# Linear attention into an ELU feed-forward, one core: first products of four chunks, two more pairs transposed by DMA, one set of PSUM banks, and a new order of work

## The chip, the cores and the metric

The kernel runs on one core of one Trainium2 chip. The metric is the device time of one execution in microseconds (us), the median of several runs. TensorE (PE) multiplies matrices from SBUF into PSUM, which has eight banks; VectorE (DVE) and ScalarE (ACT) read PSUM and write SBUF; GpSimd (POOL) computes in SBUF and issues the loads that change the type; SyncE (SP) issues the other transfers, the stores and the transposes by DMA.

## The reference

Four sequences of 768 tokens with eight heads of 64 go through a linear attention with decay, in blocks; its output, 3072 rows of 512, goes through two dense layers with an ELU between them. Cut to what matters:

```python
intra = einsum('bhic,bhjc->bhij', qb, kb) * Dmask          # scores within a block, masked by decay
intra = einsum('bhij,bhjd->bhid', intra, vb)
inter = einsum('bhid,bhde->bhie', qb * lam_pow, kv_state)   # what earlier blocks left
out   = intra + inter
kv_state = lam_block * kv_state + einsum('bhsd,bhse->bhde', kb * rev_pow, vb)
...
x = out.transpose(0, 2, 1, 3).reshape(B * S, H * D)         # 3072 x 512
h = x @ w_in                                                # 512 x 2048
g = where(h > 0, h, exp(min(h, 0)) - 1)
return g @ w_out                                            # 2048 x 512
```

## The kernel before

**The pieces.** The work is cut into 24 chunks of 128 tokens. Chunk g is block g // 4 of sequence g % 4, so chunk g needs the state that chunk g - 4 left. Everything is multiplied in float16 and summed in PSUM in float32.

**The order.** A long string, PROGRAM, holds one word for each step, and the loop at line 453 carries the words out one after another. Since each engine works through its own instructions in order, the words of one engine make that engine's queue. The text behind an @ names the PSUM bank or banks that the word takes. The words, with the chunk numbers behind the letters:

- Lq, Lk, Lv (load, line 238): POOL issues the load of one chunk, or from chunk 4 on of a pair, from float32 in memory to float16 in SBUF. wi and wo (lines 244, 250) load a block of 256 columns of the first weight, or 256 rows of the second, eight of each. Hq and Hk (line 225) load a chunk as float32 over SP's queue, and Cq or Ck (line 231) casts it.
- T, Tq, Tk (transpose, line 259): TensorE transposes q and k of a chunk, four matmuls for each against the identity; tq (DVE, which also multiplies by the decay qs) and tk (ACT, unless named in ON) copy the result to qT and kT. Dq and Dk (transpose_dma, line 278): SP issues a DMA that does the same without TensorE, DVE or ACT; the decay qs then comes in later, in p.
- S (scores, line 282): the scores of a chunk, 16 small matmuls in two banks; s (masked, line 292): DVE multiplies one half by the mask.
- P (products, line 298): masked scores times values plus q times state, in one bank; p (evacuate_p, line 315) copies it to xt, the input of the dense layers: on ACT if q came by tq, on DVE with the factor qs if it came by Dq.
- kd (POOL) and U (TensorE) make what a chunk adds to the state, M (POOL) decays the old state, u (DVE) adds the two.
- A (first_product, line 385): 128 x 512 of the first dense layer's output, in a bank. x (ACT) takes the exponential of it, r (ACT) the maximum with 0 in place, m (DVE) puts the two together as g. A chunk has 2048 columns of hidden layer. A group of n chunks shares its A words: four words for each chunk alone (16 matmuls of 128 columns each), eight words for a pair (eight matmuls of 256 columns each). GROUPS names the groups.
- B (second_product, line 416): a quarter of the second dense layer of one chunk, four matmuls of 512 columns; o copies the sum to osb, st (SP) stores it. Of the last chunk, 384 columns go this way and the last 128 in R, oR and stR.

**The banks.** Before, A takes the two buffers of bank H in turn; scores, products, updates and transposes share A, B, C, D; the second products take M0 and M1, and now and then another word takes one of these.

**The order around the change.** Chunks 0 to 3 go alone. T4 to T7 stand on TensorE, with their copies on DVE and ACT. Words A and B alternate from the start: the first A is A0:0, the first B is B0:0, two A later. Around the first product of chunk 4 the order reads:

```
B2:3 A3:1 S4@M0,B M4 Lk10 S5@A,M1 Lq10 M5 s4.0 s5.1 s4.1 x3:1 A3:3 o2 x3:3 s5.0 kd7 r3:3
T6@D B3:0@M0 P4@C P5@B p4 p5 m3:3 B3:3 A4:0 r3:1 Lv6 tk6 m3:1 tq6 Dq8 Dq9 Dk9 x4:0 r4:0
```

POOL's loads stand in this order: wi1, then q, k, v of the first chunks with wi0, wo0, wo1, wi2, wi3 among them, then the other weights, then Lq4 Lk4 Lk6 Lq6 Lv4 Lq8 and so on. A tile's buffers (BUFS) bound how far a load can run ahead: four for each of q, k, v in pairs, five for qT and for kT, 40 for g.

Of the kernel before, what the change touches and what calls it, by code (L numbers as in the profile page):

```python
# [11 lines left out]
ALU = mybir.AluOpType  # L12


GROUPS = [(0, 1), (1, 1), (2, 1), (3, 1), (4, 2), (6, 2), (8, 2), (10, 2), (12, 2), (14, 2), (16, 2), (18, 2), (20, 2), (22, 2)]

LOADS = [(0, 1), (1, 1), (2, 1), (3, 1), (4, 2), (6, 2), (8, 2), (10, 2), (12, 2), (14, 2), (16, 2), (18, 2), (20, 2), (22, 2)]

BUFS = {'qn1': 4, 'kn1': 4, 'vn1': 4, 'qn2': 4, 'kn2': 4, 'vn2': 4, 'qT': 5, 'kT': 5, 'pp': 6, 'kd': 8, 'stt': 8, 'xt1': 4, 'xt2': 2, 'xt4': 2, 'e': 3, 'g': 40, 'osb512': 4}

ON = {'z0.0', 'z2.0', 'z1.0', 'o23', 'z3.0'}

# [4 lines left out]


PROGRAM = (
# [53 lines left out]
)  # L85


# [1 line left out]
def kernel(  # L89
# [11 lines left out]
    nc = tc.nc  # L101
# [57 lines left out]
        return sb.tile(shape, dtype, tag=tag, name=name, bufs=BUFS.get(tag, 1))  # L159

    def bank(tag, shape, dtype, name):
        return ps.tile(shape, dtype, tag=f"ps{tag}", name=name, bufs=2 if tag == "H" else 1)

    def ln(_):
        nc.scalar.activation(loglam[:], lam_b[:], AF.Ln)
# [216 lines left out]
                out=new, in0=stt.pop((g, hh))[r], in1=psU.pop((g, hh)), op=ALU.add  # L382
            )

    def first_product(g0, j):
        n = size_of[g0]
        assert {f"p{g0 + i}" for i in range(n)} <= done
        pH = psH[g0, j] = bank("H", [128, FB * 128], FP32, f"psH{g0}_{j}")
        for f in range(FB // n):
            i, w = divmod(j * (FB // n) + f, 2)  # L390
            for kk in range(NHP):
                nc.tensor.matmul(  # L392
                    pH[:, f * n * 128 : (f + 1) * n * 128],
                    lhsT=wi16[i][:, kk, w * 128 : (w + 1) * 128],
                    rhs=xg[g0][:, kk, :], start=(kk == 0), stop=(kk == NHP - 1),
                )
# [38 lines left out]
        t0 = b * S + c * L  # L435
        nc.sync.dma_start(out=out[t0 : t0 + 128, cols], in_=osb.pop((g, cols.start))[:])

    rest = []

    def last_columns(banks):  # L440
        cols = slice(CUT, DM)
# [11 lines left out]
    for word in words:  # L453
# [17 lines left out]
        elif kind in ("Dq", "Dk"):  # L471
            transpose_dma(kind[1], *a)
        elif kind == "S":
            scores(*a, banks)
        elif kind == "P":
            products(*a, banks)
        elif kind == "U":
            update_products(a, banks)
        elif kind == "B":
            second_product(*a, banks)  # L480
        elif kind == "o":
            evacuate_o(*a, psM.pop(*a)[:, cols_of(*a)], cols_of(*a), name in ON)
        elif kind == "st":
            store(*a, cols_of(*a))
        elif kind == "R":
            last_columns(banks)
        elif kind == "oR":
            evacuate_o(LAST, rest[0][:], slice(CUT, DM), False)
        elif kind == "stR":
            store(LAST, slice(CUT, DM))  # L490
        else:
            {
                "wi": load_wi, "wo": load_wo, "z": zero_state, "s": masked, "p": evacuate_p,
                "kd": decay_k, "M": decay_state, "u": update, "A": first_product, "x": exp,
                "r": relu, "m": elu,
            }[kind](*a)

# [29 lines left out]
```

## Time and profile before

| what | value |
|---|---|
| median of 3 runs (lowest to highest) | 215.63 us (215.39 to 217.02) |
| the profiled execution | 215.01 us |
| its span, first to last instruction | 213.2 us |
| granted clock of TensorE, mean | 1.000 |
| first matmul, first A | 6.13 us, 14.39 us |
| x, mean of 96, ACT (line 400) | 596 ns |
| r, mean of 96, ACT (line 403) | 594 ns |
| m, mean of 96, DVE (line 408) | 685 ns |
| s, mean of 48, DVE (line 294) | 682 ns |
| transposes by DMA, issue to landing, median | 5.1 us for qT, 4.1 us for kT |
| loads of a pair, POOL's issue, mean | 1.1 us |

The span is what the trace covers; the device time is some 1.8 us longer. Busy times of TensorE are modelled ends of matmuls that overlap, so the cost of a matmul is read from the distance between starts: a chain entry such as "16 matmuls in 1.75 us" gives it, the mean duration does not. A DMA share over 1 means that more than one packet was under way on each engine.

### The profile page before, as it was taken

The numbers are of one execution on the slowest core, as the hardware profiler recorded it, in microseconds if no ns is written. First come the engines' busy times: TensorE is split into PE (matmuls) and PEld (weight loads), VectorE is DVE, ScalarE is ACT, GpSimd is POOL, SyncE is SP. The second block draws the span as 40 slices with busy tenths as digits, with TensorE's granted clock in tenths as the row PEclk, the third lists the DMA queues.
The fourth block names the chain that finished last, engine by engine and source line by source line (L and its number), as shares of the span: only waits on it lengthen the run. The fifth ranks groups of instructions, "written<-read, shape, count | busy, mean of one in ns | idle before, by whom it ended". The sixth has DMA issues, their size and how long they took to land.

```text
span 213.2 us, 5052 instructions
## 1 busy us (share of the span) xinstructions
PE 199.2 (93%) x2048; PEld 138.5 (65%) x2048; DVE 129.6 (61%) x223; ACT 127.9 (60%) x245; POOL 96.6 (45%) x115
## 2 busy tenths in 40 slices
PE   0599989999999999999989999999999999999994
PEld 0378767677677766767657677667666776666662
DVE  3877764385877866788538676366558665353321
ACT  4436766568776765585554865665674565556731
POOL 7999965599994995376902691000000000000000
PEclk9999999999999999999999999999999999999999
DMA  5999999999999999969997999146110000021042
GB/s 95 152 181 184 197 194 182 158 145 151 161 120 166 127 169 150 148 101 113 187 148 80 158 187 127 25 130 145 25 52 0 0 16 36 3 103 46 0 152 98
DMA packets 101976, 24.59 MB, mean 115 GB/s; under 512 B 92608, under 2 KB 99008, under 8 KB 101952
## 3 DMA queue, kind: packets, MB, share of 16 engines
q0 software_dynamic: 79760, 13.50, 83.5%
q1 hardware_dynamic: 22192, 10.76, 23.9%
q8 instruction: 16, 0.26, 0.5%
q14 instruction: 8, 0.07, 0.1%
HBM read 27.27 MB, written 6.29 MB: 157 GB/s over the span
## 4 chain that ended last, share of the span: by engine, by line
PE 64%; POOL 17%; DMA 15%; issue 1%; ACT 0%; SPq 0%; POOLq 0%
PE psM L422 29%; PE psH L392 28%; DMA kn<-in_k_dram 5%; DMA vn<-in_v_dram 4%; DMA qT<-qn 4%; POOL wi L245 3%; POOL kn L240 3%; POOL wo L251 3%; POOL kd L332 3%; DMA out_dram<-osb 3%; POOL qn L240 3%; PE psO L304 2%; POOL vn L240 2%; PE psO L310 2%; PE psS L287 2%
## 5 line engine op out<-in xcount | busy, mean ns | idle before, releaser
L408 DVE SCALAR_TENSOR_TENSOR g<-e,psH 128x512 f16<-128x512 f32 x96 | 65.6, 685 | 61.3 <-ACT psH L403 61.0
L392 PE MATMUL psH<-xt,wi 128*128 128x256 f16 (+1 forms) x896 | 97.6, 259 | 0.9 <-DMA wi<-in_moe_w_in_dram 0.8
L400 ACT ACTIVATE e<-psH 128x512 f32<-128x512 f32 x96 | 57.2, 596 | 67.4 <-PE psH L392 67.0
L422 PE MATMUL psM<-wo,g 128*128 128x512 f16 (+1 forms) x384 | 92.7, 377 | 0.2 <-ACT osb L431 0.2
L392 PEld LDWEIGHTS <-wi 128*128 128x128 f16 x896 | 77.5, 99 | 22.8 <-DMA wi<-in_moe_w_in_dram 1.3
L403 ACT ACTIVATE psH<-psH 128x512 f32<-128x512 f32 x96 | 56.9, 594 | 0.0
L422 PEld LDWEIGHTS <-g 128*128 128x128 f16 x384 | 36.4, 98 | 31.4 <-issue 0.4
L294 DVE TENSOR_TENSOR pp<-psS,mask 128x512 f16<-128x512 f32 x48 | 31.4, 682 | 7.6 <-PE psS L287 7.5
L332 POOL TENSOR_TENSOR kd<-kn,ks 128x512 f16<-128x512 f16 x20 | 20.8, 1049 | 13.0 <-DMA kn<-in_k_dram 12.5
L342 POOL TENSOR_TENSOR stt<-st,upp 64x256 f32<-64x256 f16 x32 | 19.6, 612 | 7.4 <-DVE st L381 5.9
L240 POOL DMA_DIRECT2D vn<-in_v_dram x14 | 15.7, 1121 | 9.0 <-PE psO L310 9.0
L431 ACT COPY osb<-psM 128x512 f32<-128x512 f32 x23 | 13.4, 588 | 5.7 <-PE psM L422 4.8
L240 POOL DMA_DIRECT2D kn<-in_k_dram x14 | 15.5, 1107 | 1.6 <-DMA wi<-in_moe_w_in_dram 1.4
L240 POOL DMA_DIRECT2D qn<-in_q_dram x13 | 14.4, 1110 | 0.1
L381 DVE TENSOR_TENSOR st<-stt,psU 64x256 f16<-64x256 f32 x32 | 13.0, 415 | 0.8 <-PE psU L366 0.3
L304 PE MATMUL psO<-pp,vn 128*64 128x128 f16 x192 | 12.5, 229 | 0.3 <-DMA vn<-in_v_dram 0.3
L304 PEld LDWEIGHTS <-vn 128*64 128x64 f16 x192 | 10.0, 114 | 2.6 <-issue 1.6
L328 DVE TENSOR_TENSOR xt<-psO,qs 128x512 f16<-128x512 f32 x16 | 10.7, 683 | 1.1 <-PE psH L392 0.6
L287 PE MATMUL psS<-qT,kT 64*128 64x128 f16 x192 | 8.4, 228 | 2.8 <-DMA qT<-qn 1.1
L310 PE MATMUL psO<-qT,st 128*64 128x128 f16 x160 | 10.3, 219 | 0.0
L287 PEld LDWEIGHTS <-kT 64*128 64x128 f16 x192 | 5.9, 98 | 5.8 <-issue 3.6
L310 PEld LDWEIGHTS <-st 128*64 128x64 f16 x160 | 9.0, 110 | 0.0
(45 smaller groups left out, 65.1 us busy)
## 6 DMA issues: line engine op xcount, KB each, us to landing
out_dram<-osb SPq DMA_DIRECT2D x23, 256.0 KB, 2.9
qn<-in_q_dram POOLq DMA_DIRECT2D x10, 256.0 KB, 8.0
kn<-in_k_dram POOLq DMA_DIRECT2D x10, 256.0 KB, 6.5
vn<-in_v_dram POOLq DMA_DIRECT2D x10, 256.0 KB, 7.0
wi<-in_moe_w_in_dram POOLq DMA_DIRECT2D x8, 256.0 KB, 6.4
wo<-in_moe_w_out_dram POOLq DMA_DIRECT2D x8, 256.0 KB, 7.4
kn<-in_k_dram POOLq DMA_DIRECT2D x4, 128.0 KB, 4.7
vn<-in_v_dram POOLq DMA_DIRECT2D x4, 128.0 KB, 5.5
```

The lines of the kernel that those rows point to most:

```text
L240: nc.gpsimd.dma_start(out=t[:].rearrange("p b h d -> p (b h) d"), in_=source(w, g0, load_n[g0]))
L287: nc.tensor.matmul(psS[g, hh][:, hp, :], lhsT=tr["k", g][r, hp, :], rhs=tr["q", g][r, hp, :], start=True, stop=True,)
L294: nc.vector.tensor_tensor(out=p[:], in0=psS.pop((g, hh))[:], in1=mask[:, hh::2, :], op=ALU.mult)
L304: nc.tensor.matmul(po[r, hp, :], lhsT=of("v", g)[:, 2 * hp + hh, :], rhs=pp[g, hh][:, hp, :], start=True, stop=(cb == 0), skip_group_check ...
L310: nc.tensor.matmul(po[r, hp, :], lhsT=st[b][cb % 2][:, hp, r], rhs=tr["q", g][:, hp, :], start=False, stop=True, skip_group_check=True,)
L332: nc.gpsimd.tensor_tensor(out=kds[g][:], in0=of("k", g), in1=ks[:].unsqueeze(2).broadcast_to([128, H, 64]), op=ALU.mult,)
L342: nc.gpsimd.tensor_tensor(out=t[r], in0=st[b][cb % 2][r, :, r], in1=upp[r].unsqueeze(2).broadcast_to([64, NHP, 64]), op=ALU.mult,)
L392: nc.tensor.matmul(pH[:, f * n * 128 : (f + 1) * n * 128], lhsT=wi16[i][:, kk, w * 128 : (w + 1) * 128], rhs=xg[g0][:, kk, :], start=(kk = ...
L400: nc.scalar.activation(es[g0, j][:], psH[g0, j][:], AF.Exp)
L403: nc.scalar.activation(psH[g0, j][:], psH[g0, j][:], AF.Relu)
L408: nc.vector.scalar_tensor_tensor(out=g[:].rearrange("p f c t -> p (f c t)"), in0=es.pop((g0, j))[:], scalar=-1.0, in1=psH.pop((g0, j))[:], ...
L422: nc.tensor.matmul(psM[g][:, cols], lhsT=gts[g, f], rhs=wo16[i][:, w, cols], start=f == 0, stop=f == NFT - 1, skip_group_check=True,)
```

## The change

- GROUPS: from chunk 8 on, four chunks share their first product (16 words A for a group, four matmuls of 512 columns each) instead of two. Chunks 0 to 3 stay alone, 4 to 7 stay pairs.
- Chunks 4 to 7: the words T, tq and tk are replaced by Dq and Dk. Their p goes from ACT to DVE, since the factor qs now comes in there.
- Banks: every bank is a single buffer, named 0 to 7, and every A names its bank.
- Head: a word wz sets a tile of zeros, and 14 words W multiply zeros, 13 ahead of the first transposes and one behind Tq1. Chunk 0's k comes over SP as float32 (Hk0, Ck0).
- The order of all words is new.

```diff
-GROUPS = [(0, 1), (1, 1), (2, 1), (3, 1), (4, 2), (6, 2), (8, 2), (10, 2), (12, 2), (14, 2), (16, 2), (18, 2), (20, 2), (22, 2)]
+GROUPS = [(0, 1), (1, 1), (2, 1), (3, 1), (4, 2), (6, 2), (8, 4), (12, 4), (16, 4), (20, 4)]
...
-ON = {'z0.0', 'z2.0', 'z1.0', 'o23', 'z3.0'}
+WARM = [512, 512, 512, 512, 512, 512, 512, 512, 512, 512, 512, 512, 512, 512]
+
+ON = {'z3.0', 'z0.0', 'z2.0', 'o23', 'Ck0', 'z1.0'}
...
-        return ps.tile(shape, dtype, tag=f"ps{tag}", name=name, bufs=2 if tag == "H" else 1)
+        return ps.tile(shape, dtype, tag=f"ps{tag}", name=name, bufs=1)
...
-    def first_product(g0, j):
+    def first_product(g0, j, banks):
...
-        pH = psH[g0, j] = bank("H", [128, FB * 128], FP32, f"psH{g0}_{j}")
+        pH = psH[g0, j] = bank(banks[0], [128, FB * 128], FP32, f"psH{g0}_{j}")
...
+    def make_zeros(_):
+        idle.append(const("zeros", [128, 512], FP16))
+        nc.vector.memset(idle[0][:], 0.0)
+
+    def zeros_product(k, banks):
+        if k == 0:
+            idle.append(bank(banks[0], [128, 512], FP32, "psW"))
+        nc.tensor.matmul(
+            idle[1][:, : WARM[k]], lhsT=idle[0][:, :128], rhs=idle[0][:, : WARM[k]],
+            start=True, stop=True,
+        )
```

The new order from the head to the first products of chunk 4, and its end; the middle is left out:

```
Hq0 wz W0@0 W1 W2 W3 W4 W5 wi3 W6 W7 W8 W9 W10 Lq1 iota row z3.1 pos0 idn Lk2 Lk1 Lq2 tab
lam ln Cq0 Hk0 W11 W12 pos1 dn Ck0 Tk0@1 Lk3 Lv1 Lq3 Lv2 Lv0 wi2 wi0 wi1 llp qs up pos2
Tq0@2 ks z0.0 tk0 kd1 kd0 Lv3 wi4 wi5 wi6 wo1 kd3 wi7 cau wo0 Lq4 Lk4 wo4 wo5 Lk6 wo3 wo2
Dq5 Dq4 Lq6 Tq1@3 W13 tq0 tq1 wo6 z2.1 Tk2@4 tk2 msk S0@5,6 s0.1 Tk1@7 tk1 S1@0,2 Tq2@1 tq2
S2@3,4 T3@7 U1@6 s0.0 s1.1 tk3 s2.0 s2.1 P2@1 P0@5 s1.0 z1.1 tq3 kd2 U0@2 wo7 p2 p0 P1@3 p1
z3.0 S3@4,0 Dk5 A2:1@1 x2:1 r2:1 A0:1@7 A1:1@5 x1:1 s3.0 m2:1 A1:0@3 s3.1 x1:0 r1:0 Dk4 P3@4
u1.0 A2:0@1 m1:0 u1.1 A0:0@0 Dk6 Dk7 p3 Dq6 A3:1@4 x0:1 r0:1 m0:1 r1:1 x0:0 m1:1 r0:0 x2:0
Dq7 A0:2@3 z0.1 u0.1 A1:2@6 Lv4 A3:0@7 U3@5 r2:0 m2:0 u0.0 x1:2 r1:2 m1:2 A2:2@1 x0:2 r0:2
x3:0 m0:2 r3:0 A3:2@2 m3:0 m0:0 x2:2 kd7 r2:2 m2:2 A0:3@6 x0:3 r0:3 m0:3 u3.1 A1:3@3 A3:3@7
x3:3 z1.0 A2:3@0 r3:3 m3:3 u3.0 Lk8 kd5 M5 x2:3 B1:0@1 B0:0@6 B2:0@7 B2:2 r2:3 m2:3 B1:2
x1:3 r1:3 x3:2 r3:2 m3:2 Lv6 kd6 M4 B3:0@5 B3:2 B0:2 m1:3 B1:1 x3:1 r3:1 m3:1 U2@0 u2.1 B3:1
u2.0 B2:1 B0:1 S5@2,3 S4@4,0 B1:3 B0:3 s5.0 s4.1 s4.0 s5.1 B3:3 Lq8 Lq10 kd4 P4@2 p4 P5@0 p5
U4_5@4 B2:3 M6 A4:4@3 u5.1 u5.0 u4.1 Lk10 o0 o2 M7 Lv8 u4.0 x4:4 o3 A4:1@6 x4:1 r4:1 o1 r4:4
...
A20:8@2 B20:1 B20:3 B23:3 x20:8 r20:8 m20:8 B21:2 o21 B22:2 o22 st22 B20:2 o20 st21 B23:2 st20 o23
st23 R@0 oR stR
```

In the middle, the scores of chunks 8 to 11 stand between B of chunks 4 to 7, those of 12 to 15 among the A of the group at 8, and those of 16 to 23 among the A of the group at 12 and the B of chunks 8 to 11. The 16 A of the groups at 16 and 20 come last, mixed with each other and with B of chunks 12 to 19. TensorE's queue has 32 transposing matmuls fewer, SP's has eight transposes more (40 instead of 32).

More of the change, by code (lines that the diff above doesn't have):

```diff
@@ L436, in store @@
         nc.sync.dma_start(out=out[t0 : t0 + 128, cols], in_=osb.pop((g, cols.start))[:])
-    rest = []
+    rest, idle = [], []
+    def make_zeros(_):
+        idle.append(const("zeros", [128, 512], FP16))
+        nc.vector.memset(idle[0][:], 0.0)
+    simple["wz"] = make_zeros
+    def zeros_product(k, banks):
[5 more added lines that the diff above has]
+        )
     def last_columns(banks):
@@ L478 @@
             update_products(a, banks)
+        elif kind == "A":
+            first_product(*a, banks)
+        elif kind == "W":
+            zeros_product(*a, banks)
         elif kind == "B":
@@ L493 @@
                 "wi": load_wi, "wo": load_wo, "z": zero_state, "s": masked, "p": evacuate_p,
-                "kd": decay_k, "M": decay_state, "u": update, "A": first_product, "x": exp,
+                "kd": decay_k, "M": decay_state, "u": update, "x": exp,
                 "r": relu, "m": elu,
```

109 rows, old and new, of the table PROGRAM are left out of this document.

## The prediction

> **What bounds the kernel now.** I read five views: the busy table, the chain of waits, the timeline of TensorE, the windows of the DMA-heavy stretch, and the timeline of SP's queue. The busy table first.
>
> ```profile
> PE 199.2 (93%) x2048; PEld 138.5 (65%) x2048; DVE 129.6 (61%) x223; ACT 127.9 (60%) x245; POOL 96.6 (45%) x115
> ```
>
> TensorE is the bound on average, so the question is what one of its words costs and where it stands still. The chain of waits gives the prices (start, length, what), and two landings.
>
> ```profile
> 28.72 11.07 DMA kn<-in_k_dram
> ...
> 50.37 7.86 DMA vn<-in_v_dram
> ...
> 83.00 1.73 PE psM L422 x8
> 84.73 1.75 PE psH L392 x16
> ...
> 209.22 0.91 PE psMrest L445 x16
> ```
>
> 16 matmuls of 256 columns take 1.75 us (109 ns each), 8 of 512 columns 1.73 us (216 ns each), 16 of 128 columns 0.91 us (57 ns each). So a word B costs 0.863, a two-chunk A (eight matmuls) 0.872, a one-chunk A (sixteen of 128 columns) 0.90. The keys of chunks 4 and 5 (Lk4) landed at 39.8, the values of 6 and 7 (Lv6) at 58.2. The timeline shows where TensorE starts, where chunk 4's output product P4 begins, and its named stops behind that.
>
> ```profile
> 14.39 2.80 PE L392 MATMUL psH<-xt,wi 128*128 128x128 f16 x31
> ...
> 46.96 0.25 PE L304 MATMUL psO<-pp,vn 128*64 128x128 f16 x2
> ...
> 58.28 0.25 PE L304 MATMUL psO<-pp,vn 128*64 128x128 f16 x2 [0.33 <-DMA vn<-in_v_dram]
> ...
> 107.48 0.62 PE L287 MATMUL psS<-qT,kT 64*128 64x128 f16 x16 [1.09 <-DMA qT<-qn]
> ```
>
> Behind 14 us TensorE hardly rests, and what stops it is DMA. The windows (last three columns: clock, DMA share, GB/s) and SP's queue show the DMA side.
>
> ```profile
> 30.00:36.00 6.00, 5.22 (x70) 3.95 (x69) 1.77 (x4) 3.85 (x9) 3.42 (x3) 1.00 1.48 194
> 36.00:42.00 6.00, 6.00 (x62) 4.00 (x60) 2.55 (x6) 3.04 (x7) 2.14 (x2) 1.00 2.45 158
> ...
> 46.59 3.09 SPq L280 DMA_TRANSPOSE qT<-qn  x2
> 49.77 2.60 SPq L280 DMA_TRANSPOSE kT<-kn  x2
> 55.33 6.61 SPq L280 DMA_TRANSPOSE qT<-qn  x3
> ```
>
> From 36 to 42 us only loads of pairs of chunks run: 262 KB at 158 GB/s is 1.66 us each. Weights go at 194 GB/s, 1.35 us each. The share is over 1, so the DMA engines are full: there is a second bound, as high as TensorE, to some 60 us.
>
> **The change part by part.**
>
> *Four chunks at a time.* From chunk 8 on, 64 two-chunk A words (0.872) become 64 four-chunk words of four 512-column matmuls (0.864): 0.5 us less. The number of x, r and m is the same (96 each, by 128x512 rows), so ACT and DVE gain nothing.
>
> *Chunks 4 to 7 by DMA.* TensorE loses 32 transposes of 57 ns, 1.8 us. ACT loses four tk and four p, 8 x 0.59; DVE swaps four tq for four p. SP gains eight transposes, which it issues at about 1.3 us each, and the DMA engines move them while full. Their price: from Lk4 (39.8) to Lv6 (58.2) nine pair loads landed. At 1.66 us they need 14.9 of the 18.4; 3.5 us went to the four or five transposes that ran in that time, 0.7 to 0.9 each. I take 0.8. From below the bound is 0 (they hide); from above 1.3, SP's issue time, if loads stop whenever SP transposes.
>
> *Head.* The key of chunk 0 goes over SP as float32 (256 KB, 1.35 us at the weights' rate) instead of over POOL (128 KB, 0.83): 0.5 more of DMA. POOL issues two loads before the iota where it was one, so row, identity and qs come about 0.9 later (mean of such an issue 1.1, the first ones 0.9). All four chunks' scores come before the first A: DVE has 7.9 us of work from the first tq to the first A, before 6.7. Together 0.9 + 1.2 + 0.7 for the two casts and later qs on ACT: the first A moves from 14.4 to about 17.2, with wi2 landing at 16 to 17. In exchange T3, S3, U1, U0 are done by then. The 14 zero products lie in time in which TensorE waits anyway (its first matmul was at 6.1); without that cover they would cost 14 x 0.22 to 14 x 0.43 = 3 to 6 us.
>
> *The stage up to P4.* In the new order all 16 A of chunks 0 to 3 stand first, then their B, then P4: 28.4 us of TensorE's work from the first A, so TensorE would be at P4 at 45.6, and 46.5 with the slower first matmuls that before shows too. But P4 needs Lv4. In before it landed at 39.8 + 3 x 1.66 = 44.8. What POOL loads up to Lv4 is the same set in both but for chunk 0's key, and ahead of Lv4 the DMA engines now also carry six of the eight transposes (Dq5, Dq4, Dk5, Dk4, Dk6, Dk7; the other two, Dq6 and Dq7, wait for Lq6 and come with or behind Lv4). So Lv4 lands at 44.8 + 0.5 + 6 x 0.8 = 50.1. The same lateness shows earlier at B1:1 (wo2) and B1:3 (wo7), and that is one wait, not three. Everything on TensorE's queue stands behind it. P4 starts at 50.1 (46.5 if transposes cost nothing, 53.1 at 1.3 each).
>
> *Behind P4.* I summed the TensorE words. Before: 79 B and 4 short ones, 80 A, 20 P (0.45), 18 S (0.23), 8 U (0.24), T7 and R: 156.9. After: two B fewer, no T7, 64 A cheaper: 154.2. From 46.96 to the end of R (210.1) before took 163.1, so 6.2 was lost: 1.1 and 0.3 in the stops above, some 0.4 on a bank, and 4.4 in small change between groups. The small change stays (4.2). The stop on a bank goes, with eight to choose from. The DMA stops should go too: P7 comes near 57 and Lv6 some 3.3 behind Lv4, and Dk10 to Dk15 can be issued 8 us or more before S10 and S14. New is that the first A of a four-wide group needs all four p. From S8 to A8:1 DVE has 8.6 us of work beside 9.2 of TensorE, from S12 to A12:10 11.7 beside 12.7, from S19 to A16:14 14.6 beside 14.6: I charge 0.8 for the three. The tail behind R was 213.2 - 210.1 = 3.1 and stays: five stores instead of three stand on SP in the last four microseconds, at some 0.55 us of issue each, which SP has room for but for 0.3 at most.
>
> Sum: 50.1 + 154.2 + 4.2 + 0.8 + 3.1 = 212.4 of span, 0.8 under the 213.2 of before. The profiled execution took 215.01 with 213.2 of span, 0.6 under the median of 215.63; against the median the forecast is 214.8.
>
> The Trainium skill ("DMA: Bandwidth & Descriptors", section "Latency and other measured facts") gives a DMA transpose an effective 261 GB/s; by it a transpose of 131 KB is an estimated 0.5 us and not 0.8, and the sum would be 1.8 lower. The landings of this trace say 0.7 to 0.9, and the sum goes by them. The same page, section "Issuing engines are not separate DMA queues", says that DMAs of all queues run on the same 16 engines and interleave; it speaks against a transpose that is free because SP issues it, and the landings agree.
>
> **The rivals.**
>
> *The transposes hide (faster).* For it: the loads ahead of Lv4 are mostly weights, at a higher rate than in the window where I priced the transposes. Against it: nine loads took 18.4 and not 14.9. P4 then starts at 46.5: 208.8, or 211.2 by the median. At half the price (0.4 each) P4 starts at 47.7 and the median is 212.4, still over 1% faster. 0.30; with smaller losses behind P4, 0.34 for faster.
>
> *DVE stops the four-wide groups (slower).* The margins above are 0.6, 1.0 and 0. DVE waited 7.5 us in ten waits for scores (0.75 each); two such waits in each of three stages, less the 0.8 charged, is 3.7: 218.5. It decides slower from 3.0 us on. Against it: eight banks let A and B be placed freely between. 0.12.
>
> *Transposes stop the loads altogether (slower).* At 1.3 each, and all eight ahead of Lv4, P4 starts at 44.8 + 0.5 + 10.4 = 55.7: 220.4. Six at 1.3 give 53.1 and 217.8, which is at the 1% line. 0.10.
>
> **How the numbers follow.** The forecast case (transposes at 0.5 to 1.1 us, up to 2 us either way behind P4) has 0.44 and gives 214.8, its own range 213.5 to 217.7. Faster by over 1% (under 213.5) 0.34, within 1% 0.44, slower 0.22; 1% is about what a measurement of this kernel tells from no change. The range is 210.8 to 218.2: it takes in most of the first rival and the near part of the second and third.
>
> **What would show it.** Right: the transposes of chunks 4 to 7 run on SP between 29 and 48 us; TensorE waits 3 to 4 us in all for wo or vn between 35 and 50; P4 near 50; 512-column psH at 216 ns; first A near 17. The first rival: P4 at 47 or sooner with no wait for DMA. The second and third rival: waits of psH or psO for DVE near 75, 95 and 130 us, or P4 behind 53. It is wrong altogether if 512-column products run slower than 216 ns, 0.1 us for each of 64 words being 6.4 us.

## The result, and the profile after

The changed kernel takes 219.86 us (median of four runs, 219.25 to 220.79) against 215.51 of the kernel before in the same session: a ratio of 1.026, 95% interval 1.022 to 1.030. It is slower. The forecast was 214.8 us with a range up to 218.2, so the measured time lies outside the range, on the side of the third rival (transposes that hold the loads up). Executions in a slower state of the chip (a few of the kernel before, two of four in e6, and one of twelve in e9, 353 us at a granted clock of 0.56) are left out of the times and ratios of the experiments below; e6 and e9 were profiled in it.

The profiled execution has a span of 217.6 us where the forecast summed to 212.4. Here is where the 5.2 us lie.

First the busy table of the changed kernel, and what its TensorE waited for (total us, times, longest).

```profile
PE 202.7 (93%) x1774; PEld 114.1 (52%) x1774; DVE 127.8 (59%) x224; ACT 121.2 (56%) x238; POOL 95.4 (44%) x114
```

```profile
PE psM L428 <- DMA wo<-in_moe_w_out_dram: 4.4, 3, 2.6
PE psTk L270 <- ACT kn L240: 1.6, 1, 1.6
PE psS L293 <- ACT kT L282: 1.6, 2, 0.9
PE psS L293 <- DMA kT<-kn: 1.2, 1, 1.2
```

TensorE has 274 matmuls fewer and yet the same share of a longer span. What it waits for by DMA is the second weight, wo, and once a key transposed by DMA. The timeline puts these waits in their places (start, length, matmuls, and in brackets the idle time ahead of them).

```profile
18.42 4.36 PE L398 MATMUL psH<-xt,wi 128*128 128x128 f16 x64
...
34.01 7.07 PE L428 MATMUL psM<-wo,g 128*128 128x512 f16 x32
43.66 1.86 PE L428 MATMUL psM<-wo,g 128*128 128x512 f16 x4 [2.58 <-DMA wo<-in_moe_w_out_dram]
...
50.37 0.59 PE L428 MATMUL psM<-wo,g 128*128 128x512 f16 x2 [0.68 <-DMA wo<-in_moe_w_out_dram]
52.12 2.32 PE L428 MATMUL psM<-wo,g 128*128 128x512 f16 x10 [1.16 <-DMA wo<-in_moe_w_out_dram]
54.37 0.25 PE L310 MATMUL psO<-pp,vn 128*64 128x128 f16 x2
...
98.17 0.62 PE L293 MATMUL psS<-qT,kT 64*128 64x128 f16 x16 [1.20 <-DMA kT<-kn]
```

The first A starts at 18.42 (before 14.39), and P4, the output product of chunk 4, at 54.37 (before 46.96). Between them stand the three waits for wo. The chain of waits says the same and gives the prices of words (start, length, what).

```profile
32.52 19.56 DMA wo<-in_moe_w_out_dram
52.08 0.04 issue
52.12 2.32 PE psM L428 x10
...
206.26 0.86 PE psH L398 x4
207.12 5.62 PE psM L428 x28
212.74 0.91 PE psMrest L466 x16
```

One weight block, issued at 32.52, is under way for 19.56 us. Four matmuls of 512 columns for four chunks take 0.86 us, 215 ns each, as forecast. Last come SP's queue and the windows (last three columns: clock, DMA share, GB/s).

```profile
30.55 2.63 SPq L286 DMA_TRANSPOSE qT<-qn  x2
33.22 10.41 SPq L286 DMA_TRANSPOSE kT<-kn  x4
49.46 2.51 SPq L286 DMA_TRANSPOSE qT<-qn  x2
```

```profile
13.00:20.00 7.00, 6.42 (x74) 5.11 (x74) 4.88 (x9) 2.56 (x5) 7.00 (x9) 0.52 1.76 184
34.00:36.00 2.00, 2.00 (x14) 0.94 (x11) 1.33 (x4) 2.00 (x5) 0.89 (x1) 1.00 1.77 181
36.00:38.00 2.00, 2.00 (x11) 0.93 (x10) 0.69 (x2) 2.00 (x5) 0.00 (x0) 1.00 1.57 114
...
40.00:44.00 4.00, 1.42 (x6) 0.50 (x5) 0.00 (x0) 0.00 (x0) 3.44 (x4) 0.95 1.75 100
44.00:48.00 4.00, 4.00 (x16) 1.81 (x15) 0.84 (x2) 0.00 (x0) 3.78 (x6) 0.62 1.46 181
...
50.00:52.00 2.00, 0.59 (x2) 0.19 (x2) 1.99 (x4) 0.00 (x0) 1.93 (x3) 1.00 4.87 76
```

The eight new transposes are issued from 30.55 to 51.97. In that time the DMA engines are engaged (share over 1) but move 114 GB/s from 36 to 38 us, 100 from 40 to 44 and 76 from 50 to 52, where the kernel before moved 194 and 158 GB/s from 30 to 42 us with no transpose on the way. TensorE's clock is granted by half from 13 to 20 us (0.52) and again behind the first stop (0.62 from 44 to 48).

Against the forecast's sum: P4 came at 54.37 and not at 50.1 (+4.3); from there to the end of R it took 213.65 - 54.37 = 159.3, forecast 159.2; the tail is 217.6 - 213.65 = 3.95 and not 3.1 (+0.85). So the miss lies almost wholly ahead of P4.

### The profile page after: what moved, and what is told of

The parts are those of the page before. It is cut to its first block, busy times and chain, and to the rows that moved or that the text cites. A ratio compares the mean times of both kernels' runs of the same rounds, so it can differ in the third digit from the quotient of the medians.

```text
span 217.6 us, 4446 instructions
## 1 busy us (share of the span) xinstructions
PE 202.7 (93%) x1774; PEld 114.1 (52%) x1774; DVE 127.8 (59%) x224; ACT 121.2 (56%) x238; POOL 95.4 (44%) x114
## 4 chain that ended last, share of the span: by engine, by line
PE 67%; DMA 17%; POOL 10%; DVE 2%; SPq 1%; issue 1%; ACT 0%; POOLq 0%
PE psM L428 30%; PE psH L398 29%; DMA wo<-in_moe_w_out_dram 9%; DMA qn<-in_q_dram 4%; DMA kT<-kn 4%; POOL wi L251 3%; PE psO L310 2%; PE psS L293 2%; PE psO L316 2%; POOL kd L338 2%; POOL vn L246 2%; POOL qn L246 1%; POOL kn L246 1%; PE psU L372 1%; POOL wo L257 1%; DVE st L387 1%
## 5 line engine op out<-in xcount | busy, mean ns | idle before, releaser
L414 DVE SCALAR_TENSOR_TENSOR g<-e,psH 128x512 f16<-128x512 f32 x96 | 63.3, 684 | 55.3 <-ACT psH L409 54.8
L428 PE MATMUL psM<-wo,g 128*128 128x512 f16 (+1 forms) x384 | 88.7, 381 | 4.4 <-DMA wo<-in_moe_w_out_dram 4.4
L398 PE MATMUL psH<-xt,wi 128*128 128x128 f16 (+2 forms) x640 | 88.6, 296 | 0.0
L398 PEld LDWEIGHTS <-wi 128*128 128x128 f16 x640 | 52.0, 99 | 32.2 <-issue 0.2
L428 PEld LDWEIGHTS <-g 128*128 128x128 f16 x384 | 37.1, 99 | 47.9 <-issue 6.3
L409 ACT ACTIVATE psH<-psH 128x512 f32<-128x512 f32 x96 | 55.9, 600 | 0.0
L300 DVE TENSOR_TENSOR pp<-psS,mask 128x512 f16<-128x512 f32 x48 | 30.3, 683 | 7.8 <-PE psS L293 7.7
L348 POOL TENSOR_TENSOR stt<-st,upp 64x256 f32<-64x256 f16 x32 | 19.5, 608 | 9.8 <-DVE st L387 8.2
L246 POOL DMA_DIRECT2D vn<-in_v_dram x14 | 15.5, 1114 | 5.5 <-PE psO L316 5.1
L334 DVE TENSOR_TENSOR xt<-psO,qs 128x512 f16<-128x512 f32 x20 | 13.0, 686 | 5.1 <-PE psO L316 5.1
L246 POOL DMA_DIRECT2D kn<-in_k_dram x13 | 14.5, 1114 | 1.4 <-issue 1.0
L246 POOL DMA_DIRECT2D qn<-in_q_dram x13 | 14.5, 1116 | 0.7 <-DMA wo<-in_moe_w_out_dram 0.6
## 6 DMA issues: line engine op xcount, KB each, us to landing
wo<-in_moe_w_out_dram POOLq DMA_DIRECT2D x8, 256.0 KB, 13.2
```

Source lines behind the costliest of these rows:

```text
L246: nc.gpsimd.dma_start(out=t[:].rearrange("p b h d -> p (b h) d"), in_=source(w, g0, load_n[g0]))
L300: nc.vector.tensor_tensor(out=p[:], in0=psS.pop((g, hh))[:], in1=mask[:, hh::2, :], op=ALU.mult)
L348: nc.gpsimd.tensor_tensor(out=t[r], in0=st[b][cb % 2][r, :, r], in1=upp[r].unsqueeze(2).broadcast_to([64, NHP, 64]), op=ALU.mult,)
L398: nc.tensor.matmul(pH[:, f * n * 128 : (f + 1) * n * 128], lhsT=wi16[i][:, kk, w * 128 : (w + 1) * 128], rhs=xg[g0][:, kk, :], start=(kk = ...
L409: nc.scalar.activation(psH[g0, j][:], psH[g0, j][:], AF.Relu)
L414: nc.vector.scalar_tensor_tensor(out=g[:].rearrange("p f c t -> p (f c t)"), in0=es.pop((g0, j))[:], scalar=-1.0, in1=psH.pop((g0, j))[:], ...
```

## The experiments

**Theory A**: the eight extra DMA transposes make the loads late in the stage in which DMA is full; TensorE then waits for wo, v and kT until P4, and what else is gained ahead of P4 is lost in that wait. **Rival B**: the four-wide groups, or the new order behind P4, cost the time. **Rival C**: the head does (first A 4 us later, clock by half, zero products).

**e1: chunks 4 to 7 on TensorE again.**

```
- Dq4 Dq5 Dq6 Dq7 Dk4 Dk5 Dk6 Dk7
+ T5@3 T4@0 tk5 tq5 tk4 tq4      (ahead of B1:1)
+ T6@2 T7@0 tk6 tq6 tk7 tq7      (behind B2:3)
```

> The changed kernel with chunks 4 to 7 transposed on TensorE again (T, tq, tk back, no Dq or Dk for them), all else as changed. Theory A (the eight DMA transposes hold up the loads ahead of P4): without them wo7 lands near 43 and Lv4 near 45, TensorE does not wait for wo, P4 starts at 47.5 to 48.5 instead of 54.4, half of the 1.8 us of transposes comes behind it; span 211 to 212.5, ratio to the kernel before 0.990 to 0.997. Theory B (the new order itself, all A ahead of all B, asks for wo too early or too late whatever the transposes): the wait for wo stays at 3 us or more, P4 at 51 or later, ratio 1.01 or more. Theory C (the half clock costs the time, not the loads): the half clock of the first 20 us stays and the ratio is 1.01 or more.

218.61 us, ratio 1.018 (1.015 to 1.022). wo7 landed at 44.1 and Lv4 at 45.8, as expected, and no wait for DMA is left; but P4 came only at 51.8. What TensorE waits for is now

```profile
PE psTk L269 <- ACT kn L239: 2.3, 1, 2.3
PE psS L292 <- ACT kT L281: 1.6, 2, 1.0
...
PE psU L359 <- DVE qT L277: 0.7, 1, 0.7
PE psS L292 <- DVE st L386: 0.7, 1, 0.7
```

The DMA waits are the transposes' doing. But most of the time stays: the first A is at 20.2 here, the clock is granted by half ahead of it (0.55 and 0.50 in the windows from 10 to 20 us), and the last two waits come from where I put the copies. So the transposes are not all of it. (TensorE's words ahead of the first A are the same in the changed kernel, e1, e2, e4, e10 and e13, but their profiles have it at 18.4, 20.2, 19.5, 19.6, 19.9 and 19.6 us: the head of a single profile is not exact to a microsecond.)

**e2: the last two weight blocks ahead of the pairs.**

```
- ... wo0 Lq4 Lk4 wo4 wo5 Lk6 wo3 wo2 ... Lq6 ... wo6 ... wo7
+ ... wo0 wo4 wo5 wo3 wo2 wo6 wo7 Lq4 Lk4 Lk6 Lq6
```

> The changed kernel with one move on POOL's queue: wo6 and wo7 ahead of Lq4, Lk4, Lk6, Lq6, so that every weight is asked for before the first transpose can start. Theory A: wo7 lands near 38, no B waits; the transposes now hold up only q, k and v of chunks 4 to 7, P4 starts at 50 to 52; ratio 1.000 to 1.012. If a transpose costs the loads the same wherever it stands and P4 is bound by Lv4 alone: Lv4 lands at 53 to 54 as now, P4 at 54, ratio 1.02 to 1.028. Theory B (order) expects no gain either.

216.69 us, 1.014 (1.007 to 1.021). The waits for wo are gone (wo7 lands at 36.6 and not at 52.1); in their place stands

```profile
PE psS L292 <- DMA kT<-kn: 1.4, 2, 0.8
```

P4 comes at 51.8. The transposes now run beside pair loads alone, and they cost less: from 34 to 53.6 us the load packets need 13.3 us at the rates of the undisturbed loads (156 KB a microsecond for pairs, 201 for weights), so 6.3 us went to eight transposes, 0.79 each. The same count on the changed kernel gives 8.8 us for six, 1.47 each.

**e3: the kernel before, with eight more transposes** of chunks 4 to 7 into tiles that nobody reads.

```
+ Xq5 Xq4 (behind Lq4)  Xk5 Xk4 (behind Lk4)  Xk6 Xk7 (behind Lk6)  Xq6 Xq7 (behind Lq6)
```

> The kernel before with eight more DMA transposes on SP's queue: q and k of chunks 4 to 7 into spare tiles that nothing reads, each behind its load; TensorE keeps its own transposes and the order. The output is that of the kernel before. Theory A: the loads behind Lk4 slip by 0.8 to 1.4 us for each transpose, Lv4 lands at 49 to 53 instead of 44.8, P4 starts 3 to 6 us later, ratio 1.012 to 1.03. Theories B and C (the transposes are harmless in themselves): ratio 0.998 to 1.004.

225.54 us, 1.053 (1.047 to 1.060), more than expected, and not where it was expected: Lv4 came at 47.1 (expected 49 to 53) and P4 at 47.2, hardly later than before, and the loss lies behind them. Only transfers were added, and TensorE stands still:

```profile
PE psO L304 <- DMA vn<-in_v_dram: 8.6, 1, 8.6
...
PE psS L287 <- DMA qT<-qn: 2.3, 1, 2.3
```

Lv6 lands at 66.7 and not at 58.2, 8.5 us for eight transposes: 1.06 each. The clock then fell by half (0.50 from 61 to 71 us). This is the plainest proof that the transposes are not free.

**e4: the changed kernel with pairs from chunk 8 on**, as GROUPS had it before.

> The changed kernel with pairs again in the first product from chunk 8 on: every four-chunk A, x, r, m becomes the pair word of the same bank in the same place, six buffers for the pairs' input. Theory A: 64 words at 0.872 instead of 0.864, 0.5 us more, ratio 1.025 to 1.030 to the kernel before. If the four-chunk products are what costs (a wait of theirs or a slower 512-column product): ratio 1.015 or less.

222.31 us, 1.036 (1.032 to 1.040).

```profile
57.86 0.25 PE L308 MATMUL psO<-pp,vn 128*64 128x128 f16 x2
```

P4 comes at 57.86 here and not at 54.37, though ahead of it the two kernels have the same words. Behind P4 the span has 162.5 us left with pairs and 163.2 with groups of four. So what these two profiles differ by is not a gain of the four-wide groups, and the 0.5 us forecast for them is not shown. What rival B's first half needed, a loss of some 5 us in them, is not there either.

**e5: transfers alone.** No kernel of the reference: its output is zeros.

> The disputed price by itself, nothing else is computed and the output is zeros: five phases one after another, each waiting for the one before: eight loads of a block of w_out (256 KB each as float16), eight loads of a pair of chunks of q (256 KB each), eight DMA transposes of a 128x512 tile, eight weight loads beside eight transposes, eight pair loads beside eight transposes. Theory A as predicted: a transpose takes 0.8 us from loads of either kind, so weights go from 10 to 11 us alone to 17 to 18, pairs from 13 to 14 to 20. Theory A as the changed kernel suggests (Lv4 8.5 us later for six transposes, beside weights; 0.8 each in the run with weights first, beside pairs): weights lose 1.2 to 1.5 us for each transpose, 20 to 23 us in all, pairs 0.7 to 0.9. Theories B and C: the loads beside transposes are at most 10% longer.

Eight weight loads take 14.5 us from the first issue to the last landing, beside transposes 18.8. By then 5.9 of the eight transposes had been moved, going by the bytes of their packets: 0.73 us each. (All eight as divisor, as e11's expectation has it, gives 0.53, which is too low.) The pair loads beside transposes ran into the stores of the output, so that phase says nothing. The theory had expected more beside weights; e11 takes it up.

**e6, e7, e8: the head.** e6 adds 17 zero products where TensorE waits in the head, e7 takes all zero products out, e8 is e2 with the filled head.

```
e6: + W x6 ahead of Tk0, x4 ahead of S0, x3 ahead of S1, x4 ahead of S2
e7: - wz W0 ... W13
```

> The changed kernel with 17 more zero products in the gaps of the head: six ahead of Tk0, four ahead of S0, three ahead of S1, four ahead of S2. Theory A (the loads bind until P4): the half clock between 10 and 20 us goes, the first A comes up to 1 us sooner and runs at full rate, but wo6 and wo7 land near 52 all the same; ratio 1.02 to 1.03 to the kernel before. Theory C (half clock): 2 us or more faster than the changed kernel, ratio 1.015 or less.

> The changed kernel without the tile of zeros and the 14 zero products. Theory A: no difference from the changed kernel beyond 0.5%, ratio 1.02 to 1.03, since the loads bind. Theory C: slower or faster by over 1% as the half clock lies differently in the head.

> Weights ahead of the pairs on POOL's queue (the run that came to 1.0136) and the 17 more zero products of the head. With the wait for wo gone, TensorE binds from the head on, so that here the clock must show: theory A with the head behind it: the first A's 3 us at half rate go, 1.5 to 2.5 us gained, ratio 1.000 to 1.008. If the head doesn't bind there: ratio 1.010 to 1.018.

e6: 219.9 us (two executions), 1.026 (1.014 to 1.038). e7: 221.27, 1.032 (1.023 to 1.041). e8: 216.60, 1.010 (1.003 to 1.017). Neither more zeros nor none changes the time of the changed kernel by more than the intervals allow, though in the profiles of e6 and e7 the clock is granted in full from 13 to 20 us (1.00, where the changed kernel has 0.52). In e8 the first A comes at 17.64 (19.50 in e2), and the gain ends in

```profile
PE psS L293 <- DMA kT<-kn: 4.1, 1, 4.1
```

where e2 waited 1.4. As long as the transposes stand ahead of P4, a faster head only waits longer: rival C cannot be the cause there.

**e9: transposes on TensorE and the filled head together**, the copies placed so that nothing waits for them; e14 gives the same kernel's profile.

```
- Dq4 Dq5 Dq6 Dq7 Dk4 Dk5 Dk6 Dk7
+ T5@2 T4@3 tk5 tq5 (ahead of B1:1)   tk4 tq4 (ahead of U2)
+ T6@2 T7@0 (ahead of M6)   tk6 tq6 (behind o2)   tk7 tq7 (behind u4.0)
+ the 17 zero products of e6
```

> The changed kernel without its eight extra transposes by DMA (chunks 4 to 7 on TensorE again, their copies placed so that no bank and no state waits for them), and with 17 more zero products in the head so that the clock stays granted. Theory A (the loss is the transposes by DMA plus a slow head): the transposing version alone was 4.0 us over the kernel before; the filled head moved the first A by 1.9 us where it was tried, and some 1.5 us of small waits of that version go: 0.6 us over the kernel before, ratio 1.003, between 0.995 and 1.010. Rival C (the new order itself loses the time behind P4, whatever the head): the ratio stays near 1.018.

> The same kernel as in e9, for its profile. Theory A: no wait for wo, vn, kT or qT before P4, first A at 17.5 to 18, P4 near 49, and a clock granted in full from the head on; the rest of the distance to the kernel before lies in the head. Rival: waits for DMA of over 1 us remain before P4.

215.0 us, ratio 1.002 (0.998 to 1.005), and 214.52 in the one run of e14. All of the loss is back, as theory A with a slow head said. e6 and e9 have the same filled head and differ in who does the eight transposes (1.026 against 1.002): that is what they cost more by DMA than on TensorE, with an interval of over a point to either side on e6. With the DMA out of the way the filled head counts: e1 and e9 differ by 1.7 points, of which a part belongs to the better placed copies (1.5 us of small waits in e1). In e14's profile what TensorE waits for is

```profile
PE psTk L270 <- ACT kn L240: 0.9, 1, 0.9
PE psO L310 <- DVE pp L300: 0.9, 2, 0.5
PE psM L428 <- DVE g L414: 0.9, 1, 0.9
```

and no DMA ahead of P4. So rival B's second half (which e9's expectation calls C) falls too: the new order behind P4 costs nothing that can be measured.

**e10: half the dose** (k on TensorE, q by DMA), **and e13: one transpose** (q of chunk 5 alone).

> The changed kernel with k of chunks 4 to 7 transposed on TensorE again and only q by DMA: four extra transposes by DMA instead of eight. Theory A (each transpose delays the loads): waits for wo and vn before P4 fall by half or more, from 4.7 us to under 2.4, P4 near 52, and the time lies between the two ends, 218 to 219.5 us (ratio 1.015 to 1.023). Rival D (it is the number of loads and their order, not the transposes): the waits stay near 4.7 us and the ratio at 1.026.

> The changed kernel with a single extra transpose by DMA (q of chunk 5); the other seven are on TensorE. What is read is the time from the landing of the sixth weight block wo5 to that of Lv4: 10.5 us with none ahead of it, 14.2 with two, 19.1 with six. Theory F (a burst of transposes costs a fixed stop of some 2 us where it meets weight loads, and 0.8 for each): 13.0 to 13.8. Rival L (a price in proportion, 1.4 to 1.8 each): 11.9 to 12.4.

e10: 216.2 us, 1.009 (1.005 to 1.013), better than expected; the wait for wo is 1.0 us instead of 4.4. It is also faster than e1, which has no transpose by DMA there: behind P4 e10 takes 162.5 us and e1 164.9, and this difference comes with the q transposes and copies that e1 does on the engines. So the price of a transpose can't be read from these ratios. e13: one run, 218.47 us, near e1, whose head and copies it has. What counts is the time from the landing of wo5 to that of Lv4, with so many transposes landed between, all from the trace's landings:

| transposes ahead of Lv4 | kernel | wo5 | Lv4 | apart |
|---|---|---|---|---|
| 0 | e1, e14 | 35.2, 35.3 | 45.8, 45.2 | 10.5, 9.9 |
| 1 | e13 | 35.0 | 48.2 | 13.2 |
| 2 | e10 | 35.0 | 49.2 | 14.2 |
| 6 | the changed kernel | 34.7 | 53.8 | 19.1 |

The first costs 2.7 us or more, the five behind it 1.2 each: here there is a stop that does not grow with the number, as theory F of that run had it. It is seen in the packets: with one transpose (e13) the packets under way between 36.8 and 37.7, of loads and transpose alike, took up to 1.24 us where 0.03 (128 bytes) and 0.10 (1 KB) are usual, and all ended within 0.05 us of 38.05. The changed kernel has the same at 36.2 to 37.5, and again, up to 0.69, ending at 42.05; the kernel before, at its first transposes, at 50.0 to 51.1; e1 and e14 have no such packet ahead of P4. It does not belong to every burst: in e2, whose eight transposes meet pair loads alone, no packet of a load or a transpose took over 0.40 us from the first issue to the last landing (38.3 to 54.1). And one part of sixteen comes late. A load lands in sixteen parts; those of Lk6:

| kernel | 8th part | 12th | 15th | 16th |
|---|---|---|---|---|
| e1 (no transpose) | 35.4 | 35.8 | 36.4 | 37.0 |
| e13 (one) | 35.1 | 35.7 | 36.2 | 40.3 |
| changed | 35.2 | 36.3 | 39.5 | 40.5 |

In e13 the fifteenth part of Lv4 landed at 45.9, where e1 has 45.4, and the sixteenth at 48.2, where e1 has 45.8: by then nearly all that is left of the 2.7 us is in one part. What stops the sixteenth part by four microseconds was not found; the loads behind it land behind it. In the changed kernel, with more transposes, several parts are late.

**e11: transfers alone again**, the stores held back; its output is zeros.

> No kernel of the reference: only transfers, its output is zeros. Phases, each finished before the next: eight pair loads; eight pair loads beside eight transposes; four pair loads and four weight loads in turn; the same beside eight transposes; eight weight loads beside eight transposes. Theory A1 (the price of a transpose depends on the loads beside it, pairs being more sensitive than weights): last landing of the pair loads 8 to 11 us later beside the transposes (1.0 to 1.4 each), of the mixed loads 6 to 11 later, of the weights 4.3 later as measured before (0.53 each). Rival A2 (about 0.5 us each whatever the loads, and the rest in the kernel comes from something else): 4 to 5 us later in all three.

From the first issue to the last landing: pair loads 17.3 us alone, 23.4 beside eight transposes (0.76 each); pairs and weights in turn 15.5 and 22.1 (0.82 each); weights beside transposes 18.2, against 14.5 alone in e5, with 6.0 of the eight moved by then (0.62 each). The expectation of 1.0 to 1.4 beside pairs fell. With nothing else running, a transpose costs 0.6 to 0.8, whichever loads it meets.

**e12 and e15: the head, on top of e9.** e12 loads chunk 0's k by POOL again, with iota first, and drops six of the zero products; e15 also moves the loads of q1, k1 and k2 ahead of wi3.

```
e12: - Hk0 Ck0 W14 ... W19        + iota Lk0 wi3 (behind W5)
e15: wi3 ... Lq1 ... Lk2 Lk1 Lq2  ->  Lk0 Lq1 Lk1 Lk2 wi3 Lq2
```

> The version of the run before (transposes of chunks 4 to 7 on TensorE, filled head) with chunk 0's k loaded by POOL again, as in the kernel before: iota first, then this load, then the weight block that stood first; six of the 17 extra zero products go, since the key comes sooner. Theory H (the float32 key over SP and its cast hold the first key transpose, and with it the whole head): the first key transpose comes 1 to 1.5 us sooner, the first A near 16.5 instead of 17.7, and the ratio goes from 1.002 to about 0.995 (0.990 to 1.000). Rival I (DVE's work on the four chunks' scores sets the first A): the first A stays at 17.3 or later and the ratio at 1.002.

> As e12, with the loads of q and k of chunk 1 and k of chunk 2 issued straight behind that of k of chunk 0, the weight block wi3 behind them. In e12 the first key transpose came 2.7 us sooner, but Tq1 then stood 2.25 us for its data and the first A stayed at 18.0. Theory H2 (the head is a chain of load landings): Tq1 comes 1 us sooner, the first A near 17, ratio 0.994 (0.989 to 0.999). Rival I (DVE's and ACT's copies set the head): first A 17.6 or later, ratio 0.998.

e12: 214.06 us, 0.998 (0.994 to 1.002). The first key transpose came at 6.03 instead of 8.76, and the time went into the next wait:

```profile
8.89 0.40 PE L270 MATMUL psTq<-ident,qn 128*128 128x128 f16 x4 [2.25 <-DMA qn<-in_q_dram]
...
18.01 3.75 PE L398 MATMUL psH<-xt,wi 128*128 128x128 f16 x64
```

Theory H falls: the key alone is not what holds the head. e15: 213.85 us, 0.995 (0.992 to 0.998). q1 came 2.0 us sooner, then k2 was late (1.78), and the first A is at 17.55:

```profile
6.88 0.40 PE L270 MATMUL psTq<-ident,qn 128*128 128x128 f16 x4 [0.29 <-DMA qn<-in_q_dram]
...
9.28 0.40 PE L270 MATMUL psTk<-ident,kn 128*128 128x128 f16 x4 [1.78 <-DMA kn<-in_k_dram]
...
17.55 3.75 PE L398 MATMUL psH<-xt,wi 128*128 128x128 f16 x64
```

The first A lies nearer rival I's bound (17.6) than H2's (17), the ratio nearer H2's: the order of the loads is a part of the head, and the copies between the transposes another. It is the only version here whose whole interval lies under both kernels: four-wide groups, single banks and the new order, without the eight transposes, with the head filled and its loads in the order of use.

## Why the prediction was wrong, point by point

- *Four chunks at a time.* Right in the price: 215 ns a matmul. The gain of 0.5 us is too small to be seen in e4.
- *Chunks 4 to 7 by DMA: "I take 0.8".* This is the step that failed. As an average where transposes run beside loads, 0.8 is a good number (e11 0.76 and 0.82, e2 0.79). In the changed kernel it was 1.4: Lv4 landed at 53.8 and not at 50.1, six transposes behind 44.8 + 0.5. What was missing is a stop at the start of this burst (2.7 us with a single transpose, in e13) and 1.2 for each behind it. The upper bound of 1.3 (SP's issue time) was no bound either: it lets the loads stop only while SP issues, and the one late part of sixteen was not thought of. The prediction read its 0.8 from a stretch of pair loads; here the transposes met pair and weight loads in turn. But that alone does not explain 1.4, since e11 has 0.82 for it.
- *"One wait, not three".* Half right. They are three waits, 4.4 us in all (forecast 3 to 4). P4 was set by the last of them (wo7, landed 52.08, and ten B matmuls of 2.3 us in all that stand behind it), and not by Lv4, which had landed 0.6 us ahead of P4. The forecast put P4 straight at Lv4's landing and left these matmuls out. Not forecast: the clock by half behind the stop (0.62 from 44 to 48), in which four B matmuls took 1.86 us and not 1.03.
- *The head.* The first A came at 18.4 and not at 17.2. It was hidden behind the loads, as e8 shows, and costs only once the loads are on time (e1 against e9).
- *Behind P4.* Right: 159.3 against 159.2. Within it "the DMA stops should go" was wrong by 1.2 us (S14 and S15 waited for kT), and the charge of 0.8 for DVE ahead of the four-wide groups was not needed. That the two nearly cancel is luck.
- *The tail.* 3.95 instead of 3.1. SP had the room that I gave it: it issued the last store at 213.96, 0.02 us behind the end of its copy. But that store took 2.50 us to land, behind four others issued from 211.88 on, and 1.60 in the kernel before, behind two.
- *The rivals.* That transposes hide (0.30) is refuted by e3. That DVE stops the four-wide groups (0.12) did not happen. That transposes stop the loads (0.10) was the right direction: its case of six at 1.3 gave P4 at 53.1 and 217.8 us, a little under what came. It deserved more than 0.10: with 18.4 us for nine loads and 1.3 us of issue for each transpose, a price above 0.8 was no rarer than one below.
- *The page of the Trainium skill.* By "DMA: Bandwidth & Descriptors", section "Latency and other measured facts", the estimate was 0.5 us a transpose. The traces agree where no load runs: transposes that stood queued when the last weight load had landed came 0.41 to 0.49 us apart (e5 from 71.4 to 72.8, e11 from 115.4 to 116.7). What a transpose costs the loads beside it was more, 0.6 to 0.8 in the transfers alone and 1.4 in the changed kernel, and there the measurement decides. The section "Issuing engines are not separate DMA queues" of the same page, that all queues share the same 16 engines and interleave, agrees with e3.

What stays open: why all packets stop together when the first transpose meets loads in the changed kernel, e10 and e13, and not in e2; why one of sixteen parts comes four microseconds late; and why loads ran at 76 GB/s from 50 to 52 us in the changed kernel, with hardly a transpose packet at that time.

## What to carry to other kernels

Work moved from a busy engine to "free" DMA is paid for in the landing of every load queued beside it: before pricing it, look whether DMA is full in that stage, and who waits for the loads behind. An average price from another stretch is not a bound; one transpose alone, read at the landing of the next load that matters, shows what the first one costs there. And a gain ahead of a wait for DMA is no gain: take the late transfer away first, and only then does the head count.

## What the runs showed of the hardware that was not expected

- A single DMA transpose of 128 KB beside loads delayed the loads behind it by 2.7 us (e13); further ones by 1.2 each (the changed kernel). In that stop all packets under way end together, up to 1.24 us late. In e2 eight cost 0.79 each, and no packet took over 0.40 us.
- With transfers alone, a transpose costs weight loads 0.62 to 0.73 us, pair loads 0.76, both in turn 0.82.
- A stop of TensorE of 2.58 us was followed by a clock granted by half (0.62 from 44 to 48 us); one of 8.6 us by 0.50 from 61 to 71 (e3).
